# Halves of odd head pairs exchanged, later loads issued by GpSimd, and a new order, in a DeltaNet and MLP-mixer kernel

## The chip, the cores and the metric

The kernel runs on one core of one Trainium2 chip. The metric is the device time of one execution in microseconds (us); less is better. All arithmetic is in fp32.

## The reference

Two blocks one after the other. The first is a DeltaNet attention: four batches, eight heads, 768 positions, head dimension 48. The second is a token and channel mixer on 768 x 384 per batch. The weights of the second come as 64-bit floats and are rounded to fp32 on the chip.

```python
def _attn_ref(q, k, v, beta):
    B, H, S, D = q.shape                      # 4, 8, 768, 48
    k_n = k / (np.linalg.norm(k, axis=-1, keepdims=True) + 1e-06)
    state = np.zeros((B, H, D, D), dtype=np.float32)
    y = np.zeros_like(q)
    for t in range(S):
        kt, vt, bt = (k_n[:, :, t], v[:, :, t], beta[:, :, t, None])
        y[:, :, t] = np.einsum('bhd,bhde->bhe', q[:, :, t], state)
        v_old = np.einsum('bhde,bhd->bhe', state, kt)
        state = state + bt[:, :, :, None] * np.einsum('bhd,bhe->bhde', kt, vt - v_old)
    return y.astype(np.float32)

def _moe_ref(x, w_tok1, w_tok2, w_ch1, w_ch2):
    xt = x.transpose(0, 2, 1)
    h = np.maximum(xt @ w_tok1, 0.0) @ w_tok2        # 768 -> 256 -> 768
    u = x + h.transpose(0, 2, 1)
    h2 = np.maximum(u @ w_ch1, 0.0) @ w_ch2          # 384 -> 1536 -> 384
    return (u + h2).astype(np.float32)
```

## The kernel before

The recurrence is computed in chunks of 64 positions. A batch has 12 chunks, and `recur(t)` is one chunk of all eight heads, 48 steps in all; a unit `u` is 128 positions, two steps, so there are 24 units, six to a batch. The heads are taken as four pairs: the two heads of a pair lie on partitions 0 to 63 and 64 to 127, so that a matmul of one head uses one of the four 64 x 64 quarters of TensorE's array. Which quarter it is follows from the partitions that it reads (one half or the other) and the partitions that it writes.

For every unit there is a preparation, off the chain of steps: `load_kq` loads keys and queries (from unit 12 on as rows, `load_rows` L357, turned by DVE in `turn_rows` L366; and the keys once more in the layout `kst`, by `stacked` L401), `prep` squares kst on ACT (`ksq` L463), makes norms and scales on DVE and ACT, the scaled mask `mb` (L497, GpSimd from unit 4 on) and the scaled keys in `gm` (L514, GpSimd); `grams` multiplies keys with keys and queries (`p_g` L440) and masks the result into `gm` (L443, DVE). `to_parts`, `invert`, `from_parts` and `join` invert the triangular matrices, by way of DRAM from unit 6 on (stores L608, load L655, loads L633; matmuls `p_z` and `p_x` L748, L751, L767). `load_v` loads the values in four DMAs (L401) and scales them on GpSimd (`nrm` L411, `v_st` L414).

A step then does, with the state of the step before: `p_k`, keys times state (L790), eight matmuls of which each takes two passes; `rest` = p_k − v on DVE (L797); `p_y`, queries times state (L810), interleaved with `p_w`, inverse times rest (L814); `w_t`, a copy of p_w, on ACT (L820); `p_s`, the state's increment (L828), interleaved with the second part of `p_y` (L829); `s1`, the new state, on DVE (L837); and two copies of p_y into the mixer's input `xb` on ACT (L842). p_k reads the state of a head on the partitions of this head and writes the partitions of the same or the other half, depending on the parity of the chunk alone, so all its eight matmuls use only two of the four quarters. p_y and p_w use one pair of quarters each, as do p_s and the second p_y. Each of p_k, p_y, p_w and p_s takes one of two rotating PSUM banks; another bank belongs to the warm fillers (`p_warm` L225, L235: matmuls of zeros that keep TensorE running in the start-up).

`mixer(b)` runs when its batch's steps are done: `p_1` (L986), `p_h` (L999), transposes (`p_ut` L1009, copied to `u_t` on ACT, L1013), the first channel product in a plain form for batch 0 (`p_c` L1066) and in a form with 15 instead of 18 block products for the others (`p_r` L958, evacuated by ACT L967 and DVE L970), and the second in a form with seven instead of eight (`p_o` L1088). Its outputs are stored by SP (L1020). The weights are loaded by SP (L271), rounded by ACT, DVE and GpSimd, and kept.

Everything is written as jobs (generators), one for each unit, step, batch and weight block; a string `order` (L1162 and on) lists word by word which job takes its next piece: `k` load_kq, `p` prep, `c` and `d` the two grams, `t` to_parts, `i` invert, `f` from_parts, `j` join, `v` load_v, `r` recur, `m` mixer, `w` weights, `x`, `z` and `Y` fillers. Each engine executes its instructions in this order, and waits only for the tiles (or PSUM banks) that an instruction needs. All DMAs are issued by SP, in this order too, so a DMA that waits for a buffer holds up those behind it.

Of the kernel before, what the change touches and what calls it, by code (L numbers as in the profile page):

```python
# [13 lines left out]
C = 64  # L14
# [9 lines left out]
def kernel(  # L24
# [73 lines left out]
    def ps_seq(shape, name):  # L98
        return psum.tile(shape, FP32, name=name, tag="seq", bufs=2)
# [34 lines left out]
    G = U // HB  # L134
    pads = const.tile([128, 2, NL, H * DP], FP32, name="pads")
# [82 lines left out]

    p_warm = psum.tile([128, 4, 128], FP32, name="p_warm", tag="warm", bufs=1)
# [122 lines left out]
    ranked = set()  # L342
    spread = set()
    keyed = set()

    def load_rows(u, i, src):
# [6 lines left out]
            "(p par) (s g) d -> par s p (g d)", par=2, g=G  # L353
        )
        for par in range(2):
            for r, f in ((C * par, 0), (C * par + HB, HB)):
                nc.sync.dma_start(  # L357
                    out=rows_of[i][r : r + HB, :, 0 : G * D - f], in_=rows[par, :, :, f:]
                )
                if r == C + HB:  # L360
                    spread.add((i, u))
                yield
# [9 lines left out]
    def load_kq(u):  # L372
        b, c = divmod(u, NCH)
        kst = kst_of[slot(u)]
        if u >= TU:
            yield from load_rows(u, 0, k)
            assert last_in(u) in ranked
            yield from stacked(kst, k, u)
            yield from load_rows(u, 1, q)
            return  # L380
        for pad, src in ((kpad, k), (qpad, q)):
# [4 lines left out]
            )  # L386
            yield
            if src is k and u >= RU:
                yield from stacked(kst, k, u)

        heads = kpad[slot(u)].rearrange("t (p par) d -> t p par d", par=2)
        for cc in range(2 if u < RU else 0):
            for par in range(2):
                nc.scalar.copy(kst[PAR[par ^ cc], :, cc], heads[PAR[cc], :, par, 0:D])
                yield

    def stacked(dst, src, u):
        rows = heads_of(src, u)
        for par in range(2):
            for cc in range(2):  # L400
                nc.sync.dma_start(  # L401
# [32 lines left out]
    def grams(u, cc):  # L434
        kqt = kqts[place(u)]
        p_g = ps_prep([128, NP, 2, C], "p_g")
        for p in range(NP):
            for i in range(2):
                f = PAR[i] if u < TU else FEATS[i]
                nc.tensor.matmul(p_g[PAR[i ^ cc], p], kqt[f, p, cc, 0], kqt[f, p, cc])  # L440
            yield
        assert before_in(u) is None or 2 * before_in(u) + cc in walked
        nc.vector.tensor_tensor(  # L443
            out=blocks(gm_of(u))[:, :, cc, D:GW].rearrange(
                "s p (two n) -> s p two n", two=2
            ),
            in0=p_g,
            in1=made[u][:, :, cc, None, :].to_broadcast([128, NP, 2, C]), op=ALU.mult,
        )
        grammed.add((u, cc, False))  # L450
        yield

    def prep(u):
# [7 lines left out]

        ksq = work.tile([128, NB, D], FP32, name="ksq", bufs=1)
# [816 lines left out]
```

## Time and profile before

| | us |
|---|---|
| median of 3 runs | 639.93 (639.85 to 643.66) |
| the profiled execution | 638.03 |
| its span | 636.3 |

The span is the time from the first to the last instruction that the profile shows; 1.7 us of the execution lie around it. The profiled execution is 1.9 us below the median of the runs. The engines are called PE (TensorE), DVE (VectorE), ACT (ScalarE), POOL (GpSimd) and SP (SyncE, which only issues DMAs). PEclk is the granted clock of TensorE as a share of full speed. Where the profile writes "x16" behind a matmul, it counts passes: an fp32 matmul is recorded twice.

### The profile page before, as it was taken

The page shows a single profiled execution, that of the slowest core. Times are in us where ns is not written, and L with a number is a line of the kernel's source. Part 1 is how long each engine was busy: PE and PEld are TensorE (multiplying, and loading weights), DVE is VectorE, ACT ScalarE, POOL GpSimd, SP SyncE. Part 2 cuts the span into 40 slices and gives each one's busy share as a digit, 9 for nine tenths or more (in the row PEclk, how much of TensorE's full clock was granted, in tenths as well). Part 3 has the DMA queues.
Part 4 walks back from the last instruction along what each step waited for, and adds up shares of the span by engine and source line. Part 5 has one row for each costly group of instructions (what it writes and reads, how often), then busy time and mean ns, then how long its engine had stood idle before and what let it go on. Part 6 is the DMA issues. An engine that isn't in the chain of part 4 may idle for free.

```text
span 636.3 us, 21488 instructions
## 1 busy us (share of the span) xinstructions
PE 606.3 (95%) x9132; PEld 529.0 (83%) x9132; DVE 447.3 (70%) x1132; ACT 259.5 (41%) x631; POOL 108.7 (17%) x146
## 2 busy tenths in 40 slices
PE   8488798899999999999999999999999999999997
PEld 5367676667898988958999999769999987999997
DVE  4987876966899568988969987785627253373643
ACT  7758886447422242125623333135244230223240
POOL 2348364235301113021110010101010000000000
PEclk9878997899999999999999999999999999999999
DMA  9787568646442444354444033202020000000000
GB/s 201 131 145 170 138 133 206 151 111 155 104 111 60 92 110 92 81 131 79 92 103 101 13 94 49 66 10 38 2 54 2 27 2 0 26 1 26 1 26 26
DMA packets 135776, 50.27 MB, mean 79 GB/s; under 512 B 114656, under 2 KB 130144, under 8 KB 135680
## 3 DMA queue, kind: packets, MB, share of 16 engines
q1 hardware_dynamic: 135680, 48.89, 34.5%
q8 instruction: 72, 1.18, 0.8%
q14 instruction: 24, 0.20, 0.1%
HBM read 39.42 MB, written 9.44 MB: 77 GB/s over the span
## 4 chain that ended last, share of the span: by engine, by line
PE 81%; DVE 7%; ACT 5%; DMA 3%; issue 2%; SPq 1%; POOL 0%; DVEq 0%; ACTq 0%; POOLq 0%
PE p_o L1088 26%; PE p_r L958 19%; PE p_c L1066 7%; PE p L986 5%; PE p_h L999 5%; PE p_k L790 3%; PE p_s L828 3%; PE p_g L440 3%; PE p_y L810 3%; DMA d<-in_moe_w_ch_dram 1%; PE p_z L748 1%; PE p_ut L1009 1%; PE p_w L814 1%; DVE sub L661 1%; PE p_y L829 1%
## 5 line engine op out<-in xcount | busy, mean ns | idle before, releaser
L1088 PE MATMUL p_o<-wc,r 128*128 128x192 f32 x720 | 125.8, 329 | 0.6 <-ACT u_t L1013 0.6
L1088 PEld LDWEIGHTS p_o<-wc,r 128*128 128x128 f32 x720 | 116.7, 190 | 2.7 <-ACT u_t L1013 1.1
L970 DVE TENSOR_TENSOR r<-r,p_r 128x512 f32<-128x512 f32 x90 | 59.7, 684 | 39.9 <-PE p_r L958 38.8
L1017 DVE TENSOR_TENSOR xb<-xb,p_o 128x192 f32<-128x192 f32 x84 | 29.3, 350 | 59.5 <-PE p_o L1088 59.3
L967 ACT COPY r<-p_r 128x512 f32<-128x512 f32 x54 | 31.5, 584 | 91.4 <-PE p_r L958 89.8
L666 DVE TENSOR_TENSOR x<-x,sub 128x84 f32<-128x84 f32 (+24 forms) x178 | 59.6, 335 | 6.1
L661 DVE TENSOR_TENSOR sub<-x 128x84 f32<-128x84 f32 (+24 forms) x178 | 58.4, 328 | 7.1 <-DMA x<-n_dram 2.8
L1066 PE MATMUL p_c<-u_t,wc 128*128 128x256 f32 x216 | 51.2, 387 | 0.2 <-ACT u_t L1013 0.2
L1088 PE MATMUL p_o<-wc,s 128*128 128x192 f32 x288 | 50.5, 329 | 0.3 <-DVE xb L1017 0.3
L414 POOL TENSOR_TENSOR v_st<-v_st,nrm 128x384 f32<-128x384 f32 x24 | 20.6, 859 | 174.6 <-DMA v_st<-in_v_dram 140.7
L1088 PEld LDWEIGHTS p_o<-wc,s 128*128 128x128 f32 x288 | 46.8, 190 | 1.2 <-DVE xb L1017 0.6
L820 ACT COPY w_t<-p_w 128x192 f32<-128x192 f32 x48 | 15.3, 319 | 73.2 <-PE p_w L814 72.5
L1066 PEld LDWEIGHTS p_c<-u_t,wc 128*128 128x128 f32 x216 | 39.6, 190 | 5.9 <-ACT u_t L1013 0.4
L974 ACT ACTIVATE r<-r 128x512 f32<-128x512 f32 x54 | 33.8, 630 | 25.6 <-DVE r L970 25.3
L440 PE MATMUL p_g<-kq 48*64 48x128 f32 (+1 forms) x704 | 38.3, 290 | 3.3 <-ACT kq L509 3.3
L497 POOL TENSOR_TENSOR mb<-mask_c,cs 128x512 f32<-128x512 f32 x20 | 21.0, 1050 | 114.1 <-DVE gm L443 45.1
L842 ACT ACTIVATE xb<-p_y 64x192 f32<-64x192 f32 x96 | 31.1, 324 | 21.3 <-PE p_y L829 10.5
L958 PE MATMUL p_r<-u_t,wc 128*128 128x128 f32 x288 | 38.5, 277 | 0.0
L958 PE MATMUL p_r<-t_d,wc 128*128 128x128 f32 x288 | 37.2, 280 | 0.0
L443 DVE TENSOR_TENSOR gm<-p_g,mb 128x512 f32<-128x512 f32 x44 | 29.4, 683 | 10.0 <-PE p_g L440 7.2
L986 PE MATMUL p<-xb,w 128*128 128x384 f32 x96 | 35.6, 513 | 0.0
L958 PEld LDWEIGHTS p_r<-u_t,wc 128*128 128x128 f32 x288 | 35.3, 192 | 0.3
(177 smaller groups left out, 1200.1 us busy)
## 6 DMA issues: line engine op xcount, KB each, us to landing
d<-in_moe_w_ch_dram SPq DMA_DIRECT2D x24, 384.0 KB, 3.9
v_st<-in_v_dram SPq DMA_DIRECT2D x96, 48.0 KB, 2.5
out_dram<-xb SPq DMA_DIRECT2D x23, 192.0 KB, 1.9
kst<-in_k_dram SPq DMA_DIRECT2D x64, 48.0 KB, 3.2
n_dram<-gm SPq DMA_DIRECT2D x72, 32.0 KB, 2.4
pads<-in_k_dram SPq DMA_DIRECT2D x24, 96.0 KB, 2.4
pads<-in_q_dram SPq DMA_DIRECT2D x24, 96.0 KB, 2.5
gm<-w_dram SPq DMA_DIRECT2D x72, 32.0 KB, 2.1
```

Source lines behind the costliest of these rows:

```text
L440: nc.tensor.matmul(p_g[PAR[i ^ cc], p], kqt[f, p, cc, 0], kqt[f, p, cc])
L661: nc.vector.tensor_tensor(out=tmp, in0=y[:, :, 0:s, s : s + 1].to_broadcast([n, k, s, w]), in1=y[:, :, s : s + 1, s + 1 : m].to_broadcast( ...
L666: nc.vector.tensor_tensor(out=y[:, :, 0:s, s + 1 : m], in0=y[:, :, 0:s, s + 1 : m], in1=tmp, op=ALU.add,)
L842: nc.scalar.mul(y[:, :, D * i : D * i + D], p_y[PAR[1 - i]], 1.0 if c else -1.0)
L958: nc.tensor.matmul(p[:, i], pieces[i // width][:, at : at + 128], f[f"u{n}"], start=first and i == 0, stop=True, skip_group_check=True,)
L967: nc.scalar.copy(o, p)
L970: nc.vector.tensor_tensor(out=o, in0=o, in1=p, op=ALU.add if sign > 0 else ALU.subtract)
L974: nc.scalar.activation(o, o, ACTF.Relu)
L986: nc.tensor.matmul(p_1[dh], piece_of(w1, c, 0)[:, dh * 128 : (dh + 1) * 128], xb[:, c], start=(c == 0), stop=(c == NCH - 1),)
L999: nc.tensor.matmul(p_h, piece_of(w2, j, c * 128)[:, c * 128 : (c + 1) * 128], r1[j], start=(j == 0), stop=(j == NDH - 1),)
L1066: nc.tensor.matmul(p_c[:, k], piece_of(wc1, cb, f * 128)[:, f * 128 : (f + 1) * 128], u_t[:, cb], start=(cb == 0), stop=(cb == NCB - 1),)
L1088: nc.tensor.matmul(p, a[:, m], wc2[:, m, j], start=(start and i == 0), stop=(i == NM - 1), skip_group_check=True,)
```

## The change

Five things change together.

- **PSUM.** The two rotating banks and the fillers' bank become one tile `seq` of three banks; the fillers write bank 2. For units below 12 p_k, p_w and p_s use bank 1 and p_y bank 0. For units 12 to 23 p_k lies in banks 0 and 1 (even pairs in 0, odd pairs in 1), p_y likewise, p_w in bank 2, p_s in banks 1 (even) and 2 (odd).
- **Exchanged halves.** For units 12 to 23 the two heads of an odd pair change sides in the key and query tiles: `load_rows` writes head and partition half crosswise, in eight DMAs of half the size instead of four. The p_k matmuls of even and odd pairs then lie on different quarters, four in all. The grams, mb (two instructions on halves instead of one, 12 more on GpSimd in all), the layout of gm and the y copies follow this; no other instruction is added.
- **GpSimd issues** the loads of v from unit 6 on (72 DMAs) and those of kst from unit 12 on (48 DMAs), which SP issued before. With the 96 more of load_rows, SP issues 24 fewer DMAs.
- **A new order string**, the same up to the preparation of unit 3 and then sorted anew. It has 21 more filler matmuls (4671 matmuls instead of 4650): seven more of 512 columns, two more of 128, twelve more of the small ones. Some of them stand around the p_k of step 9 (the second pair of lines at the end of the diff; in the first pair, the same place of the old order).
- Assertions on the order (`keys_in`, `pads_in`, `held`), which make no instruction.

```diff
-    def ps_seq(shape, name):
-        return psum.tile(shape, FP32, name=name, tag="seq", bufs=2)
+    seq = psum.tile([128, 3, 512], FP32, name="seq", bufs=1)
+    p_warm = seq[:, 2].rearrange("s (m n) -> s m n", m=4)
+
+    def ps_seq(bank):
+        n = NP * D
+        return seq[:, bank, 0:n].rearrange("s (j odd d) -> s j odd d", odd=2, d=D)
+
+    def ps_split(bank, at):
+        n = NP // 2 * D
+        return seq[:, bank : bank + 2, at * n : at * n + n].rearrange(
+            "s odd (j d) -> s j odd d", d=D
+        )
...
     def load_rows(u, i, src):
-            "(p par) (s g) d -> par s p (g d)", par=2, g=G
-        )
-        for par in range(2):
-            for r, f in ((C * par, 0), (C * par + HB, HB)):
-                nc.sync.dma_start(
-                    out=rows_of[i][r : r + HB, :, 0 : G * D - f], in_=rows[par, :, :, f:]
-                )
-                if r == C + HB:
-                    spread.add((i, u))
-                yield
+            "(j odd par) (s g) d -> odd par s j (g d)", par=2, odd=2, g=G
+        )
+        for odd in range(2):
+            for side in range(2):
+                for r, f in ((C * side, 0), (C * side + HB, HB)):
+                    nc.sync.dma_start(
+                        out=rows_of[i][r : r + HB, odd:NP:2, 0 : G * D - f],
+                        in_=rows[odd, side ^ odd, :, :, f:],
+                    )
+                    if odd and r == C + HB:
+                        spread.add((i, u))
+                    yield
...
     def load_kq(u):
-            yield from stacked(kst, k, u)
+            for n, _ in enumerate(stacked(kst, k, u, nc.sync if u < 12 else nc.gpsimd)):
+                if n == 3:
+                    keys_in.add(u)
+                yield
...
+    def stacked(dst, src, u, queue):
         rows = heads_of(src, u)
         for par in range(2):
             for cc in range(2):
-                nc.sync.dma_start(
+                queue.dma_start(
                     out=dst[PAR[par ^ cc], :, cc], in_=rows[par, cc]
                 )
...
     def load_v(u):
         vsts[u] = v_st = loads.tile([128, NP, 2, D], FP32, name="v_st")
-        yield from stacked(v_st, v, u)
+        yield from stacked(v_st, v, u, nc.sync if u < 6 else nc.gpsimd)
...
     def grams(u, cc):
+        odd = u >= SWAP
         for p in range(NP):
             for i in range(2):
                 f = PAR[i] if u < TU else FEATS[i]
-                nc.tensor.matmul(p_g[PAR[i ^ cc], p], kqt[f, p, cc, 0], kqt[f, p, cc])
-            yield
-        assert before_in(u) is None or 2 * before_in(u) + cc in walked
+                half = cc ^ (odd and p % 2)
+                nc.tensor.matmul(
+                    p_g[PAR[i ^ cc], p], kqt[f, p, half, 0], kqt[f, p, half]
+                )
...
+        out = gm_of(u)[:, :, D:GW]
+        if odd:
+            picked = slice(0, 4, 3) if cc == 0 else slice(1, 3)
+            out = out.rearrange("s (j n) c -> s j n c", n=4)[:, :, picked].rearrange(
+                "s j q (two n) -> s j q two n", two=2
+            )
+            p_g = p_g.rearrange("s (j q) two n -> s j q two n", q=2)
+            mb = sorted_of(made[u])[:, cc, :, :, None, :].to_broadcast(
+                [128, NP // 2, 2, 2, C]
+            )
+        else:
+            mb = made[u][:, :, cc, None, :].to_broadcast([128, NP, 2, C])
...
     def prep(u):
+        if u < SWAP:
+            scaler.tensor_tensor(
+                out=mb, in0=mask_c[:, None, None, :].to_broadcast([128, NP, 2, C]),
+                in1=cs[:, :, :, None].to_broadcast([128, NP, 2, C]), op=ALU.mult,
+            )
+        else:
+            shape = [128, NP // 2, 2, C]
+            of = cs.rearrange("s (j odd) c -> s j (odd c)", odd=2)
+            for cc, picked in enumerate((slice(0, 4, 3), slice(1, 3))):
+                scaler.tensor_tensor(
+                    out=sorted_of(mb)[:, cc],
+                    in0=mask_c[:, None, None, :].to_broadcast(shape),
+                    in1=of[:, :, picked, None].to_broadcast(shape), op=ALU.mult,
+                )
...
     def recur(t):
...
-        heads = [(p, i, PAR[i ^ cc], PAR[1 - i]) for p in range(NP) for i in range(2)]
+        odd = u >= SWAP
+        heads = [
+            (p, i ^ (odd and p % 2), PAR[i ^ cc], PAR[1 - i ^ (odd and p % 2)])
+            for p in range(NP) for i in range(2)
+        ]

         if c > 0:
-            p_k = ps_seq([128, NP, D], "p_k")
+            p_k = ps_split(0, 0) if odd else ps_seq(1)
             for p, i, r, _ in heads:
                 f = FEATS[i]
-                nc.tensor.matmul(p_k[r, p], kqt[f, p, cc, 0], s0[f, p])
-                if i == 1:
+                nc.tensor.matmul(p_k[r, p // 2, p % 2], kqt[f, p, cc, 0], s0[f, p])
+                if r == PAR[1 ^ cc] and (p % 2 or not odd):
                     if p == NP - 1:
                         keyed.add(t)
                     yield
             assert u in scaled
             rest = rest_t
             nc.vector.tensor_tensor(
-                out=rest, in0=p_k, in1=vsts[u][:, :, cc], op=ALU.subtract
+                out=split(rest), in0=p_k, in1=split(vsts[u][:, :, cc]),
+                op=ALU.subtract,
             )
             yield
         else:
             rest = vsts[u][:, :, cc]

         assert u in scaled and u in joined
-        p_y = ps_seq([128, NP, D], "p_y")
-        p_w = ps_seq([128, NP, D], "p_w")
+        p_y = ps_split(0, 2) if odd else ps_seq(0)
+        p_w = ps_seq(2 if odd else 1)
         for p, i, r, o in heads:
             if c > 0:
                 f = FEATS[i]
                 nc.tensor.matmul(
-                    p_y[o, p], kqt[f, p, cc, 1], s0[f, p],
-                    start=(p == 0), stop=False,
+                    p_y[o, p // 2, p % 2], kqt[f, p, cc, 1], s0[f, p],
+                    start=(p == 0 or odd and p == 1), stop=True,
+                    skip_group_check=True,
                 )
-            nc.tensor.matmul(p_w[r, p], gm[r, 2 * p + cc, TC], rest[r, p])
-            if c == 0 and i == 1 and p < NP - 1:
+            nc.tensor.matmul(p_w[r, p // 2, p % 2], gm[r, 2 * p + cc, TC], rest[r, p])
+            if c == 0 and r == PAR[1 ^ cc] and p < NP - 1:
                 yield
         if cc == 1:
             asked.add(u)
         yield
-        nc.scalar.copy(w_t, p_w)
+        nc.scalar.copy(split(w_t), p_w)
         yield

         on = c < NQ - 1
         if on:
-            p_s = ps_seq([128, NP, D], "p_s")
+            p_s = ps_split(1, 3) if odd else ps_seq(1)
         for p, i, r, o in heads:
             if on:
-                nc.tensor.matmul(p_s[PAR[i], p], gm[r, 2 * p + cc, 0:C], w_t[r, p])
+                nc.tensor.matmul(
+                    p_s[PAR[i], p // 2, p % 2], gm[r, 2 * p + cc, 0:C], w_t[r, p],
+                    start=(not odd or p % 2 == 1 or c == 0 and p == 0), stop=True,
+                    skip_group_check=True,
+                )
             nc.tensor.matmul(
-                p_y[o, p], gm[r, 2 * p + cc, GC], w_t[r, p],
-                start=(c == 0 and p == 0), stop=(p == NP - 1),
+                p_y[o, p // 2, p % 2], gm[r, 2 * p + cc, GC], w_t[r, p],
+                start=(c == 0 and p == 0),
+                stop=True, skip_group_check=True,
             )
         walked.add(t)
         yield
         if on:
             if c > 0:
-                nc.vector.tensor_tensor(out=s1, in0=s0, in1=p_s, op=ALU.subtract)
+                nc.vector.tensor_tensor(
+                    out=split(s1), in0=split(s0), in1=p_s, op=ALU.subtract
+                )
             else:
-                nc.vector.tensor_copy(out=s1, in_=p_s)
-            yield
-        for i in range(2):
+                nc.vector.tensor_copy(out=split(s1), in_=p_s)
+            yield
+        y = y.rearrange("s (j odd) (i d) -> s j (odd i) d", odd=2, i=2)
+        for e in range(2):
+            if odd:
+                picked = slice(0, 4, 3) if e == 0 else slice(1, 3)
+            else:
+                picked = slice(e, 4, 2)
             nc.scalar.mul(
-                y[:, :, D * i : D * i + D], p_y[PAR[1 - i]], 1.0 if c else -1.0
+                y[:, :, picked],
+                p_y[PAR[1 - e]],
+                1.0 if c else -1.0,
             )
...
     order = """
...
-    w29 w27*2 r8*2 w29*3 j4*2 r8 w22*4 t9*4 r8*3 p10 h5*2 k11 p9 r8 h5 r9 h5 j5
-    r9*4 w4 i2*2 p10 i2*2 v5 i2 v5 w19 m0 r9 k10 j5 p10 i2 p10 v5 i2*2 w15 w4 v5*2
...
+    w22 t8*3 r8*5 p10 w7 j4*2 w29*2 h5*4 r8*2 w29*2 t9*4 w22*2 p10 v6 r8 w4 Y r8
+    r9*2 j5 Y w4*2 p11*2 r9*3 p10*2 z i2 v5 h5 i2 x r8 r9*2 p10 r9 i2*5 z j5 r9
...
```

More of the change, by code (lines that the diff above doesn't have):

```diff
@@ L342 @@
     ranked = set()
+    keys_in = set()
+    pads_in = set()
+    held = {"t11": None, "zst": None}
     spread = set()
@@ L386, in load_kq @@
             )
+            pads_in.add((pad is kpad, u))
             yield
             if src is k and u >= RU:
-                yield from stacked(kst, k, u)
+                for n, _ in enumerate(stacked(kst, k, u, nc.sync if u < 12 else nc.gpsimd)):
+                    if n == 3:
+                        keys_in.add(u)
+                    yield
         heads = kpad[slot(u)].rearrange("t (p par) d -> t p par d", par=2)
@@ L870, in block_of @@
             return w_block(j, k)
+        for u in range(NL, WIDE):
+            assert slot(u) < NL or u in ranked and turned.issuperset([(True, u), (False, u)])
         a = {(j, k): (j, k) for j in range(3) for k in range(NCB)}
```

177 lines of the change are left out of this document (92 added, 85 removed).

## The prediction

> **What bounds the kernel now.** I read the page first: the busy line, then the slices with the granted clock.
>
> ```profile
> span 636.3 us, 21488 instructions
> PE 606.3 (95%) x9132; PEld 529.0 (83%) x9132; DVE 447.3 (70%) x1132; ACT 259.5 (41%) x631; POOL 108.7 (17%) x146
> PEclk9878997899999999999999999999999999999999
> ```
>
> PE is busy for 95% of the span, and the clock falls below 9 tenths only in the first 120 us or so. Then the busy time by stretches (columns: stretch, its length, then PE, PEld, DVE, ACT, POOL, the clock, DMA share, GB/s):
>
> ```profile
> 160.00:240.00 80.00, 79.95 (x1352) 70.53 (x1347) 64.39 (x163) 26.37 (x70) 12.95 (x17) 1.00 0.42 96
> 240.00:320.00 80.00, 79.60 (x1325) 66.83 (x1324) 71.37 (x174) 29.35 (x75) 14.74 (x19) 1.00 0.43 93
> 320.00:400.00 80.00, 80.00 (x1101) 76.66 (x1100) 64.54 (x169) 26.85 (x61) 7.08 (x12) 1.00 0.32 72
> ```
>
> From 160 us to 400 us PE idles 0.45 us in all. There only two things change the time: PE work that is removed, and a new wait that PE cannot fill. The start is another matter:
>
> ```profile
> 98.00:100.00 2.00, 1.04 (x37) 0.75 (x32) 0.72 (x3) 1.84 (x5) 0.98 (x2) 1.00 0.83 225
> 100.00:102.00 2.00, 1.46 (x49) 1.30 (x50) 0.72 (x2) 1.72 (x5) 1.10 (x2) 0.54 0.53 146
> 102.00:104.00 2.00, 1.54 (x36) 1.29 (x33) 1.05 (x4) 1.17 (x4) 1.58 (x3) 0.50 0.89 251
> 104.00:106.00 2.00, 2.00 (x8) 1.58 (x7) 1.07 (x6) 0.85 (x3) 0.52 (x2) 0.50 0.90 235
> 106.00:108.00 2.00, 2.00 (x39) 0.96 (x39) 1.76 (x8) 0.38 (x2) 0.00 (x0) 0.75 1.00 268
> ...
> 116.00:118.00 2.00, 1.53 (x60) 1.40 (x53) 1.83 (x6) 1.66 (x4) 0.00 (x0) 0.81 0.94 282
> 118.00:120.00 2.00, 2.00 (x36) 1.91 (x32) 1.93 (x7) 0.69 (x3) 0.35 (x1) 0.50 1.30 186
> 120.00:122.00 2.00, 2.00 (x19) 1.09 (x20) 1.94 (x4) 0.00 (x0) 1.02 (x2) 0.84 0.92 220
> ```
>
> A gap in PE's work at 98 us is followed by about half the clock, and PE then needs 2.28 us for what takes 1.49 us at full clock, as the chain that ended last shows:
>
> ```profile
> 89.87 5.33 DMA d<-in_moe_w_ch_dram
> 96.11 3.89 DMA d<-in_moe_w_ch_dram
> ...
> 105.11 2.28 PE p L986 x4
> ...
> 109.24 1.49 PE p L986 x4
> ...
> 122.96 0.67 PE p_y L829 x16
> ```
>
> The chain's pieces before the gap are loads of weights; its p_y at 122.96 is the last of step 11, the end of the first batch.
>
> **Keys times state (p_k) on four quarters.** The trace gives both prices. p_k alone, on two quarters, then the four-quarter p_y and p_w of a step (start, duration, what):
>
> ```profile
> 297.52 0.67 PE L790 MATMUL p_k<-s_t,kq 48*64 48x48 f32 x16
> 298.12 0.38 PE L958 MATMUL p_r<-t_d,wc 128*128 128x128 f32 x1
> ```
> ```profile
> 293.01 0.25 PE L810 MATMUL p_y<-s_t,kq 48*64 48x48 f32 x1
> ...
> 293.48 0.22 PE L814 MATMUL p_w<-rest,gm 64*64 64x48 f32 x1
> 293.62 0.25 PE L748 MATMUL p_z<-t,gm 32*32 32x32 f32 x4
> ```
>
> Sixteen passes (8 matmuls, two each) take 298.12 − 297.52 = 0.60 us on two quarters; 32 take 293.62 − 293.01 = 0.61 us on four. The 0.60 us are 8 rounds of about 58 ns and an entry and exit; four quarters need 4 rounds, so a p_k becomes 4 × 0.058 = 0.23 us shorter. The exchange acts in steps 24 to 47, of which 24 and 36 start a batch and have no p_k: 22 × 0.23 = 5.1 us at most. Not all of it is free: in the old order seven pairs of p_g matmuls ran in the quarters that p_k left empty:
>
> ```profile
> 302.30 0.28 PE L790 MATMUL p_k<-s_t,kq 48*64 48x48 f32 x4
> 302.37 0.28 PE L440 MATMUL p_g<-kq 48*64 48x128 f32 x2
> 302.41 0.28 PE L790 MATMUL p_k<-s_t,kq 48*64 48x48 f32 x4
> ```
>
> The p_g passes (302.37 and 302.48) follow each other every 0.11 us in a quarter, so such a pair, two passes in each of two quarters, hid 0.22 us beside p_k: 1.5 us for seven. With the other small shifts of the order (changes between tile sizes, p_g passes beside each other) the row prices summed over every matmul but the fillers give **−3.2 us**. The p_g, p_y, p_w and p_s matmuls keep their number and quarters: nothing. Only their places in PSUM change.
>
> **New waits in steps 24 to 47.** p_k now writes banks 0 and 1, where p_y and p_s of the step before lie. So ACT's two y copies wait for DVE's s1 (bank 1 is shared), and the next p_k waits for both y copies; before, s1 alone had to be done. The old rows, all engines in one stretch:
>
> ```profile
> 301.58 0.22 PE L829 MATMUL p_y<-w_t,gm 64*64 64x48 f32 x1
> ...
> 301.85 0.35 DVE L837 TENSOR_TENSOR s_t<-s_t,p_s 128x192 f32<-128x192 f32 x1 [0.17 <-PE p_y L829]
> ...
> 301.89 0.66 ACT L842 ACTIVATE xb<-p_y 64x192 f32<-64x192 f32 x2 [1.39 <-PE p_y L829]
> ```
>
> From the last p_y pass: 0.27 us to s1, 0.35 us in it, 0.05 us to ACT, 0.66 us for two copies, some 0.06 us to PE: 1.39 us, where 0.68 us were needed. What covers it is the PE work between the last p_y and the next p_k. In the new order it is short in eight places: before step 31 eight p_g matmuls on uneven quarters (0.66 us by 0.11 us a pass), before 37 and 44 a p_z/p_x block, before 29 sixteen p_g (0.88 us), before 40, 41, 42 and 45 four p_r matmuls. Their rows in the chain:
>
> ```profile
> 289.40 1.09 PE p_r L958 x8
> ...
> 293.69 0.62 PE p_z L748 x32
> ```
>
> With entry and exit these cover 0.72, 0.77 (twice), 0.94 and 1.24 (four times); the rest have over 1.6 us. Stalls: 0.67 + 0.62 + 0.62 + 0.45 + 4 × 0.15 = **+2.9 us**, if ACT and DVE are free at that moment. Below that, 0 if the bank wait falls away; above, 5 us if DVE's queue (89% busy in 240 to 320 us) makes s1 late. Queued on ACT behind a waiting y copy are r and w_t copies, which PE waits for. The old order's own stalls in this part, **−0.5 us** (the 0.45 above), go.
>
> **GpSimd's loads.** 120 loads (72 of v, 48 of kst) leave SP for POOL, and load_rows has 96 more, half as large, on SP. SP's longest waits are those of the stores for their data, which lie in the dense part:
>
> ```profile
> SPq L1020 <- DVE xb L1017: 202.1, 15, 44.2
> ```
>
> PE waited for no load there, so SP's relief is worth nothing and the extra row loads, hidden in these 202 us, cost nothing. At the start, where SP's queue is full, unit 12 alone brings eight of them:
>
> ```profile
> L357 SPq DMA_DIRECT2D pads<-in_k_dram x48: 312/430/1340, 111.6 to 345.9; - x48
> ```
>
> 8 × 0.43 = 3.4 us more stand against about 16 loads of v and kst that leave SP there (9.8 us at the 0.61 us of the row below): SP gains some 6 us, and the weights' loads keep their places in its queue. POOL issues no DMA in the old trace, so the price is bounded by rows of both engines (min/median/max ns):
>
> ```profile
> L411 POOL TENSOR_TENSOR nrm<-nrm,eps x24: 191/200/647, 52.2 to 471.6; 128x8 f32<-128x8 f32 x24
> ```
> ```profile
> L497 POOL TENSOR_TENSOR mb<-mask_c,cs x20: 1038/1042/1204, 29.0 to 377.6; 128x512 f32<-128x512 f32 x20
> ```
> ```profile
> L401 SPq DMA_DIRECT2D kst<-in_k_dram x64: 601/615/1512, 15.2 to 351.0; - x64
> ```
> ```profile
> kst<-in_k_dram SPq DMA_DIRECT2D x64, 48.0 KB, 3.2
> ```
>
> The ends are 0.20 and 1.20 us; I take SP's 0.62, the same load on the nearest queue. The last row has the landing, 3.2 us. It matters because ksq, kst's reader, stands in ACT's queue ahead of w_t and y. Laying POOL's queue out by these prices, kst is on time in seven of the twelve units; in five (14 to 17, 22) it lands 0.3 to 3 us late, since two v loads and four kst loads follow a late buffer release in one burst. ACT has 0 to 2 us of room after ksq: it runs some 2 us late in all, half of which I let reach PE: **+1.0 us** (0 at 0.30 us an issue, 8 at 1.05). mb in two halves costs POOL about 0.2 us a unit (its row against nrm's), hidden at 17% busy. The "DMA: Bandwidth & Descriptors" page of the Trainium skill, section "Latency and other measured facts", puts the first byte of GpSimd's DMAs at about 1 us against 0.6 for SP's; by it the term would be near 2, an estimate; no run shown yet can tell.
>
> **The new order at the start.** Up to step 11 the same work is due, DVE and ACT with 1 us more ahead of it. It has more warm fillers, of which the block around p_k of step 9 falls where the gap at 98 us was. The clock lost there is 2 × (0.46 + 0.50 + 0.50 + 0.25) = 3.4 us, at 116 us 2 × (0.19 + 0.50 + 0.16) = 1.7. As other chains (weights, DVE) end near there too, I take half: **−2.5 us** (bounds −5 and +3, if the fillers and the order only delay).
>
> **Sum.** 638.0 us (profiled execution: span 636.3 and 1.7 around it) − 3.2 + 2.9 − 0.5 + 1.0 − 2.5 = 635.7. The median of the runs shown lies 1.9 above that execution: 637.6, so I say 637.5.
>
> **Rivals.**
> 1. Faster: y copies and kst come in time and the start keeps its clock: 637.5 − 2.9 − 1.0 − 2.5 = 631. For it: ACT was only 34 to 37% busy from 240 to 400 us. Against: the covers above are counts of PE work, not guesses. 29%.
> 2. Slower: POOL's issue is dear, 1.2 us or so. kst then lands 3 to 9 us late in six units, ACT blocks by over 20 us in all, half reaches PE: 637.5 + 11.5 = 649. It starts above 0.65 us an issue and passes the 1% bound at about 1.1. For it: the bursts, ACT's strict order. Against: nrm's 0.20 us shows a light POOL instruction. 21%.
> 3. Issues that wait out a DVE instruction, half of this row's 684 ns more each:
>
> ```profile
> L970 DVE TENSOR_TENSOR r<-r,p_r 128x512 f32<-128x512 f32 x90 | 59.7, 684 | 39.9 <-PE p_r L958 38.8
> ```
>
> That is 0.96 an issue, 5 us more at PE: 642.5. Against it, mb stays at 1038 to 1204 ns beside a DVE at 80 to 89%. 6%. This is a rule of the Trainium skill ("SBUF — State Buffer", section "SBUF: two separate sides"): GpSimd cannot write descriptors while VectorE holds their shared port. By that rule it would come out so; the mb row shows little such blocking.
> 4. The change doesn't do what it says: two banks and exchanged halves leave p_k at 0.60 us. 637.5 + 5.1 − 1.5 = 641. Against it is p_y and p_w's row. 6%.
>
> **How the numbers follow.** The forecast has the remaining 38%. About 1% (6.4 us) is what a measurement of this kernel can tell from no change: below 633.5 is faster, above 646.3 slower. Faster: most of rival 1 and a tenth of the forecast's spread, 0.32. Slower: most of rival 2, with tails of 3 and the forecast, 0.26. Same: 0.42. The forecast's own range is 633 to 643; the range over the cases reaches down to rival 1 and 2 us of start beyond it, 629, and up to rival 2, 650.
>
> **What would show it.** p_k's 16 passes within some 0.37 us when alone; PE idle released by the y copy ahead of p_k, in the eight places; POOL DMAs near 0.6 us, and ACT's ksq waiting for kst by at most 3 us; a clock of 1.00 between 100 and 108 us. I am wrong if ksq waits add up to over 10 us, if s1 comes late behind DVE's queue, or if the end of step 11 (now 123.6 us) moves by more than 5 us.

## The result and the profile after

| | before | after |
|---|---|---|
| median (4 runs each, on one chip) | 641.77 us (639.85 to 643.66) | 673.62 us (673.12 to 677.18) |
| ratio to before, 95% interval | | 1.0494 [1.045, 1.0538] |
| the profiled execution, its span | 638.03, 636.3 | 673.12, 671.3 |

The change made the kernel 5% slower. The busy line and the clock of the page after, against those of before:

```profile
span 671.3 us, 21763 instructions
PE 624.0 (93%) x9174; PEld 534.0 (80%) x9174; DVE 449.5 (67%) x1132; ACT 259.3 (39%) x631; POOL 183.6 (27%) x278
PEclk9978969599999999979999999999999999999999
```

PE has 17.7 us more busy time and 17.3 us more idle time. To see where, I cut both spans at the same two events: the end of the y copies of step 11 (the last of batch 0) and of step 23. Before, then after (columns: stretch, length, busy PE, PEld, DVE, ACT, POOL, the clock, DMA share, GB/s):

```profile
0.00:124.30 124.30, 99.57 (x2261) 78.76 (x2262) 97.27 (x253) 88.09 (x234) 54.73 (x75) 0.90 0.76 160
124.30:248.40 124.10, 123.18 (x1988) 102.78 (x1988) 95.08 (x237) 49.88 (x128) 28.07 (x34) 1.00 0.46 105
248.40:636.30 387.90, 383.60 (x4886) 347.47 (x4884) 254.92 (x644) 121.58 (x270) 25.88 (x37) 1.00 0.19 45
```
```profile
0.00:142.60 142.60, 118.34 (x2305) 87.58 (x2306) 95.87 (x257) 90.47 (x240) 58.92 (x82) 0.87 0.63 138
142.60:269.00 126.40, 122.45 (x1984) 102.14 (x1983) 99.82 (x234) 47.75 (x121) 63.68 (x97) 1.00 0.48 108
269.00:671.30 402.30, 383.22 (x4888) 344.26 (x4886) 253.80 (x643) 121.03 (x270) 60.98 (x101) 0.99 0.18 42
```

The 35.0 us are +18.3 at the start, +2.3 in steps 12 to 23 and +14.4 in the rest. At the start PE idles as long as before (24.3 us, length less busy; 24.7 before) but is busy 18.8 us longer. 13.2 us of that are the fillers, which keep it busy for 31.1 us instead of 17.9 (passes that overlap counted once); the remaining 5.6 us go with a lower clock (0.87 for 0.90) and were not taken apart. In the rest it is busy as long as before and idles 19.1 us instead of 4.3.

What PE waits for stands in the groups of p_k, before and after (busy time and mean ns; idle time of PE just before the group, and what ended it), and in the waits after (us in total, times, longest):

```profile
L790 PE MATMUL p_k<-s_t,kq 48*64 48x48 f32 x656 | 28.0, 226 | 1.3 <-DVE s_t L837 0.9 <-ACT xb L842 0.4
```
```profile
L859 PE MATMUL seq<-s_t,kq 48*64 48x48 f32 x656 | 23.9, 229 | 18.7 <-ACT xb L925 18.0 <-DVE s_t L913 0.6
```
```profile
ACT xb L925 <- DVE s_t L913: 47.1, 20, 13.4
PE seq L859 <- ACT xb L925: 18.4, 20, 5.8
ACT xb L925 <- DMA out_dram<-xb: 10.0, 1, 10.0
```

p_k is 4.1 us cheaper, as intended, but PE now waits 18 us for ACT's y copies ahead of it, and the y copies wait for s1 on DVE. The prediction expected such waits where units 12 to 23 share a bank, from step 24 on. They are there earlier. This is the timeline at the end of step 13 (unit 6), where p_y lies in bank 0 and p_s and p_k in bank 1:

```profile
169.62 0.35 DVE L913 TENSOR_TENSOR s_t<-s_t,seq 128x192 f32<-128x192 f32 x1 [1.89 <-PE seq L904]
...
170.01 0.66 ACT L925 ACTIVATE xb<-seq 64x192 f32<-64x192 f32 x2 [1.29 <-DVE s_t L913]
...
170.72 0.26 PE L859 MATMUL seq<-s_t,kq 48*64 48x48 f32 x2 [0.60 <-ACT xb L925]
```

The y copy reads another bank than s1, and both only read `seq`; still it starts 0.04 us after s1 ends. p_k writes another bank than the copy reads, and still starts 0.05 us after the second copy. The order is that of the tile `seq` as a whole. This is no single case: of the 96 y copies of the kernel before, 26 run while an s1 runs; of the 96 of the changed kernel, none does.

At the start this takes in the fillers, which are now in the same tile. From the chain that ended last:

```profile
116.25 0.36 DVE rest L866
...
116.65 2.52 PE seq L234 x4
...
119.19 0.33 ACT xb L925
```

Fillers (L234), meant for a time in which PE has nothing to do, wait for rest on DVE, then take 2.52 us, and a y copy waits for them. In the first of these two stretches of 2 us PE idles for 1.54 us, in the second its clock is 0.50 (after; the last column but two is the clock):

```profile
114.00:116.00 2.00, 0.46 (x24) 0.32 (x16) 0.59 (x3) 1.41 (x4) 1.13 (x2) 0.96 0.13 50
116.00:118.00 2.00, 1.35 (x2) 0.83 (x3) 1.81 (x8) 0.47 (x2) 0.37 (x2) 0.50 0.00 0
```

At step 24, the first of a batch, the chain after shows the largest single gap:

```profile
291.15 0.36 DVE xb L1104
291.53 2.76 DMA out_dram<-xb
...
294.39 0.33 ACT xb L925
294.73 0.33 ACT xb L925
...
295.11 0.68 PE seq L859 x16
```

The y copies of step 24 write the xb buffer whose last store must land first. Before, the same wait was ACT's alone (its timeline):

```profile
271.84 0.66 ACT L842 ACTIVATE xb<-p_y 64x192 f32<-64x192 f32 x2 [7.73 <-DMA out_dram<-xb]
```

After, p_k of step 25 stands behind these copies: PE idles from 289.36 to 295.11, 5.75 us, and the clock falls to 0.83 in 280 to 300 us.

### The profile page after: what moved, and what is told of

Its sections match the earlier page's. It is cut to its first block, busy times and chain, and to the rows that moved or that the text cites. A ratio compares the mean times of both kernels' runs of the same rounds, so it can differ in the third digit from the quotient of the medians.

```text
span 671.3 us, 21763 instructions
## 1 busy us (share of the span) xinstructions
PE 624.0 (93%) x9174; PEld 534.0 (80%) x9174; DVE 449.5 (67%) x1132; ACT 259.3 (39%) x631; POOL 183.6 (27%) x278
## 4 chain that ended last, share of the span: by engine, by line
PE 69%; DVE 11%; ACT 6%; DMA 2%; issue 2%; SPq 0%; POOL 0%; DVEq 0%; ACTq 0%
PE p_o L1175 19%; PE p_r L1045 17%; PE p_c L1153 7%; PE p L1073 6%; PE p_h L1086 5%; PE seq L880 3%; ACT xb L925 3%; PE seq L859 2%; PE seq L899 2%; DVE sub L717 2%; DVE x L722 2%; PE p_g L465 2%; PE p_z L805 1%; PE seq L904 1%; DVE r L1127 1%
## 5 line engine op out<-in xcount | busy, mean ns | idle before, releaser
L424 POOL DMA_DIRECT2D v_st<-in_v_dram x72 | 44.7, 625 | 97.2 <-DVE rest L866 72.7
L925 ACT ACTIVATE xb<-seq 64x192 f32<-64x192 f32 x96 | 31.2, 325 | 89.3 <-DVE s_t L913 47.1
L1061 ACT ACTIVATE r<-r 128x512 f32<-128x512 f32 x54 | 33.9, 631 | 25.3 <-DVE r L1057 24.7
L859 PE MATMUL seq<-s_t,kq 48*64 48x48 f32 x656 | 23.9, 229 | 18.7 <-ACT xb L925 18.0
L859 PEld LDWEIGHTS seq<-s_t,kq 48*64 48x64 f32 x656 | 18.5, 137 | 27.0 <-ACT xb L925 22.6
L1073 PE MATMUL p<-xb,w 128*128 128x384 f32 x96 | 38.2, 551 | 0.0
L465 PEld LDWEIGHTS p_g<-kq 48*64 48x64 f32 (+1 forms) x704 | 28.6, 139 | 11.8 <-ACT kq L565 7.2
L293 POOL TENSOR_TENSOR wc<-w_f,d 128x384 uint32<-128x384 uint32 x24 | 24.6, 1028 | 47.4 <-DVE w_f L289 15.8
```

The source lines that it names most:

```text
L424: queue.dma_start(out=dst[PAR[par ^ cc], :, cc], in_=rows[par, cc])
L465: nc.tensor.matmul(p_g[PAR[i ^ cc], p], kqt[f, p, half, 0], kqt[f, p, half])
L859: nc.tensor.matmul(p_k[r, p // 2, p % 2], kqt[f, p, cc, 0], s0[f, p])
L925: nc.scalar.mul(y[:, :, picked], p_y[PAR[1 - e]], 1.0 if c else -1.0,)
L1061: nc.scalar.activation(o, o, ACTF.Relu)
L1073: nc.tensor.matmul(p_1[dh], piece_of(w1, c, 0)[:, dh * 128 : (dh + 1) * 128], xb[:, c], start=(c == 0), stop=(c == NCH - 1),)
```

## The experiments

Twelve kernels, in three groups. Each ratio is to the kernel before, run beside the group on the same chip (medians 641.59, 639.53 and 641.50 us); times of different groups are compared with these differences in mind. "The start" is the time up to the end of step 11, and the three stretches are cut as above.

**Which part of the change: the tile, the order, or the rest?** The first group crosses them. The kernel before with its sequence banks put into one tile (and, as in the changed kernel, `stop` set on every p_y matmul):

```diff
+    seq = psum.tile([128, 3, 512], FP32, name="seq", bufs=1)
+    p_warm = seq[:, 2].rearrange("s (m n) -> s m n", m=4)
...
-        return psum.tile(shape, FP32, name=name, tag="seq", bufs=2)
+        bank = 0 if name == "p_y" else 1
+        return seq[:, bank, 0 : NP * D].rearrange("s (p d) -> s p d", p=NP)
```

> The old kernel and old order with one edit: the two rotating banks and the fillers' bank become one tile of three banks (p_y in bank 0, p_k, p_w and p_s in bank 1, fillers in bank 2). Bank by bank nothing conflicts that did not before. Theory A: this alone makes it slower by 10 to 30 us, 652 to 672, with PE waiting ahead of p_k for the y copies in more than ten steps. Theory B and C: 640 to 645.

Measured: 667.79 us, 1.0421 [1.0392, 1.0449]. Its p_k group and its stretches:

```profile
L792 PE MATMUL seq<-s_t,kq 48*64 48x48 f32 x656 | 29.3, 227 | 18.2 <-ACT xb L844 18.0
```
```profile
0.00:128.80 128.80, 100.09 (x2252) 77.50 (x2252) 98.03 (x253) 88.12 (x235) 54.68 (x75) 0.91 0.74 156
128.80:260.50 131.70, 125.64 (x1996) 103.81 (x1997) 95.25 (x237) 50.16 (x127) 30.25 (x37) 1.00 0.44 98
260.50:665.00 404.50, 388.62 (x4886) 349.38 (x4884) 255.93 (x644) 121.62 (x270) 23.28 (x35) 0.99 0.19 43
```

One tile alone, with the old order, old halves and old queues, costs 26.2 us, and puts the same 18.0 us of waiting for the y copies before p_k; none of its 96 y copies runs while an s1 runs. The loss lies elsewhere than in the changed kernel: 4.5 us at the start, 7.6 in steps 12 to 23 and 16.6 in the rest, where PE is also busy 5.0 us longer, at a clock of 0.99 for 1.00. The edit also moved p_y and p_w to fixed banks, so p_k, p_w and p_s follow each other in one bank; in the order of a step they do so anyway, through rest, w_t and s1. The kernels with three tiles, below, have the fixed banks and the `stop` too: the first loses nothing in steps 12 to 23, and one in the old order has the start of before. Up to step 23 the tile is what is left.

The other way round, the changed kernel with three separate tiles up to step 23 (from step 24 on the split over two banks needs the one tile):

```diff
-    seq = psum.tile([128, 3, 512], FP32, name="seq", bufs=1)
-    p_warm = seq[:, 2].rearrange("s (m n) -> s m n", m=4)
...
+    banks = [early.tile([128, 512], FP32, name=f"seq{i}") for i in range(3)]
+    p_warm = banks[2].rearrange("s (m n) -> s m n", m=4)
```

> The new kernel and new order, but the three banks are three tiles up to step 23 and become the one tile at step 24, where the exchange begins; no instruction is added. Theory A: the start and steps 12 to 23 get back most of what they lost (18 + 2 us in the profiles): 652 to 660 us. Theory B: the start stays long: 668 to 674. Theory C: 670 to 674.

Measured: 662.12 us (656.18 to 665.75), 1.0335 [1.0255, 1.0416], 11.5 us less than the changed kernel. Its first two stretches:

```profile
0.00:130.70 130.70, 113.16 (x2305) 85.61 (x2306) 96.26 (x255) 90.12 (x240) 58.69 (x81) 0.91 0.69 151
130.70:253.90 123.20, 122.77 (x1984) 102.46 (x1984) 100.10 (x237) 47.69 (x122) 63.39 (x96) 1.00 0.49 111
```

The start loses 11.9 us of its 18.3, and steps 12 to 23 are 0.9 us shorter than before the change. The rest stays (403.3 us). Up to step 23 19 y copies run while an s1 runs, from step 24 on, in the one tile, none.

The order alone, in the code of before (SP issuing everything):

```diff
-    w29 w27*2 r8*2 w29*3 j4*2 r8 w22*4 t9*4 r8*3 p10 h5*2 k11 p9 r8 h5 r9 h5 j5
...
+    j4*2 w29*2 h5*4 r8*2 w29*2 t9*4 w22*2 p10 v6 r8 w4 Y r8 r9*2 j5 Y w4*2 p11*2
...
```

> The old kernel's code (old PSUM tiles, no exchange, SP issues all loads) with the new order of the pieces; where a job has more pieces in the new kernel, two of them are one here. Theory A (one tile): in the new kernel p_k, p_y, p_w, p_s and the fillers are parts of one PSUM tile, and the built program makes p_k wait for the y copies and the y copies for s1 in nearly every step from 1 on, not only from 24 on, and makes two fillers wait for DVE's rest; the order is harmless without these waits: 638 to 645 us. Theory B (order): the new order alone, with its 12 us of additional fillers before step 11, makes the start longer: 655 to 662 us, step 11 ending near 140 us instead of 124. Theory C (GpSimd's loads come late): as A for this kernel, about 641.

Measured: 703.09 us, 1.0961 [1.0923, 1.0998], slower than the whole change. Taken by itself this would convict the order. ACT's waits say otherwise:

```profile
ACT ksq L463 <- DMA kst<-in_k_dram: 65.9, 7, 18.8
```

The order is made for kst loads that don't queue on SP: with SP alone they come 65.9 us late in all. The run can't price the order; the second group gives it its queue.

And the changed code in the old order (two pieces of the grams set a little later, and the row loads twice as many):

```diff
-    r9*2 j5 Y w4*2 p11*2 r9*3 p10*2 z i2 v5 h5 i2 x r8 r9*2 p10 r9 i2*5 z j5 r9
...
+    r8 w22*4 t9*4 r8*3 p10 h5*2 k11 p9 r8 h5 r9 h5 j5 r9*4 w4 i2*2 p10 i2*2 v5 i2 v5
...
```

> The new kernel's code with the old order (the pieces of a load of rows doubled, two gram pieces set back by a few words, as the exchange needs it). Theory A: the waits remain, in an order that was not laid out for them: 655 to 675 us, with step 11 ending 8 to 18 us later than in the old kernel. Theory B: the start is as in the old kernel (124 us), and only the stalls from step 24 on remain: 645 to 652 us. Theory C: 665 or more, with ksq or v_st waiting over 10 us for GpSimd's loads.

Measured: 674.39 us, 1.0512 [1.0466, 1.0559], like the changed kernel, but differently made: its start is 132.8 us instead of 142.6, its steps 12 to 23 139.0 instead of 126.4. Two things cancel, which the second group takes apart.

**The second group: order, queue and exchange apart.** First, the old code with the new order, and GpSimd issuing as in the change:

```diff
-            yield from stacked(kst, k, u)
+            yield from stacked(kst, k, u, nc.gpsimd)
...
-        yield from stacked(v_st, v, u)
+        yield from stacked(v_st, v, u, nc.sync if u < 6 else nc.gpsimd)
```

> The old code (two rotating banks, own bank for fillers, no exchange) with the new order, and GpSimd issuing the loads of v from unit 6 and of kst from unit 12, as the new kernel does. Against e1_old_code_new_order (703) it shows what the new issue queue does in the new order. Theory A with C turned round (the order was laid out for two queues, and SP alone is late with kst): 638 to 648, the start some 6 us longer than in the old kernel and no stalls from step 24 on. Theory B: over 655.

Measured: 642.31 us (10 runs), 1.0035 [1.0014, 1.0055]. Order and queue together cost 0.35%, 2.8 us by the medians. The same queue in the old order (lines against the kernel above):

```diff
-    j4*2 w29*2 h5*4 r8*2 w29*2 t9*4 w22*2 p10 v6 r8 w4 Y r8 r9*2 j5 Y w4*2 p11*2
...
+    w29 w27*2 r8*2 w29*3 j4*2 r8 w22*4 t9*4 r8*3 p10 h5*2 k11 p9 r8 h5 r9 h5 j5
...
```

> The old kernel and old order with one edit: GpSimd issues the loads of v from unit 6 and of kst from unit 12. Theory A: 638 to 643, no change that can be measured, kst in time. Theory C: over 648, ACT's ksq waiting for kst in several units.

Measured: 652.43 us, 1.0204 [1.0159, 1.0249]. The chain shows how a moved load fails (start, duration, what):

```profile
157.66 1.01 POOL wc L284
158.67 0.57 POOL v_st L401
159.24 3.50 DMA kst<-in_k_dram
...
162.76 0.53 ACT ksq L463
...
163.32 0.55 DVE ksum L466
163.87 0.27 DVE s_t L837
...
164.19 0.34 PE p_k L790 x2
```

In POOL's queue kst stands behind a weight's rounding and a load of v. It lands late, ksq holds up ACT, ksum delays s1 on DVE, and PE idles 4.33 us. So queue and order belong together: each alone costs far more (652.43 and 703.09) than the pair (642.31).

Then the changed kernel with three tiles at the start, and three pieces of mixer(1) moved ahead of p_k of step 25, to cover the wait for the stores:

```diff
-    m0*2 i4*3 m0 i4 m0 i4 r24*4 j13 r24*3 m0 i4*3 m0*2 i4*2 p18 m0 r24 j13 r25*2
-    p18 k19 m1*3 p18 m1 k19*2 i4*4 m1*2 r25 k19*2 i4 r25 i4*2 k18*3 k19 i4*2 k19 i4
+    p18 m0 r24 j13 m1*3 r25*2 p18 k19 p18 m1 k19*2 i4*4 m1*2 r25 k19*2 i4 r25 i4*2
```

> The kernel with three tiles up to step 23, and in its order three pieces of the second mixer (4 us of p matmuls) moved ahead of step 25's p_k. Theory D (the store): at step 24 the y copies go into a buffer whose last stores are still under way; in the old kernel nothing on PE waited for these copies, now p_k of step 25 does, and PE idles 5.8 us there and loses clock behind it. Then this gains 4 to 7 us against e1_new_three_tiles_start: 655 to 658. If the idle only moves to the next wait: no gain, 660 to 663.

Measured: 650.20 us (648.88 to 651.71), 1.0167 [1.0139, 1.0196], 11.9 us less again, of which 2.1 may be the chips' (their kernels before differ by that). Only 3.8 us are the repair: the gap before p_k of step 25 shrank from 5.9 to 2.04 us, and the stretch after step 23 from 403.3 to 399.5. The start, in which nothing changed, was 126.9 us in this profile for 130.7, and the remaining 4 lie between the profiled executions and their medians (659.27 for 662.12, 651.71 for 650.20). So the length of one and the same start moves by about 4 us from profile to profile; a third kernel with it had 129.5.

This kernel and the old code with the new order and queue now differ by the exchange, the tile it needs from step 24 on, and the three moved pieces. Their p_k groups, each with its last stretch:

```profile
L877 PE MATMUL seq<-s_t,kq 48*64 48x48 f32 x656 | 23.1, 227 | 8.1 <-ACT xb L943 7.8 <-DVE s_t L931 0.2
...
250.20:649.70 399.50, 384.08 (x4888) 345.16 (x4886) 253.66 (x643) 121.10 (x271) 62.73 (x102) 0.99 0.17 42
```
```profile
L790 PE MATMUL p_k<-s_t,kq 48*64 48x48 f32 x656 | 27.1, 221 | 1.2 <-DVE s_t L837 1.0
...
250.20:639.50 389.30, 384.63 (x4888) 348.25 (x4886) 254.03 (x643) 121.43 (x270) 60.65 (x96) 1.00 0.17 44
```

Four quarters save 4.0 us of p_k's busy time but only 0.55 us of PE's. The clock takes the rest back, as far as an estimate goes. In windows of 1 us it falls to 0.50 twice in this stretch, for three windows each, behind gaps of PE of 2.04 us (ending at 276.49) and 2.30 us (ending at 383.30); 1 less the clock, summed over the windows, is 1.7 us each time, 3.4 together, and 3.45 are missing. Behind a gap of 2.19 us (ending at 525.18) it stays at 1.00, and in the old code it is 1.00 up to 630 us. PE's idle time (length less busy) rises from 4.7 to 15.4 us. The exchange, with its tile, costs 7.9 us by the medians.

Last, the changed code with three tiles at the start, in the old order:

```diff
-    p_warm = seq[:, 2].rearrange("s (m n) -> s m n", m=4)
+    p_warm = banks[2].rearrange("s (m n) -> s m n", m=4)
...
+    r8 w22*4 t9*4 r8*3 p10 h5*2 k11 p9 r8 h5 r9 h5 j5 r9*4 w4 i2*2 p10 i2*2 v5 i2 v5
```

> The new code with the old order (as e1_new_code_old_order, 674) and three tiles up to step 23. Theory A: the start returns to the old kernel's 124 us, and what is left is the exchange's stalls from step 24 on: 648 to 658. Theory B has the same for the start but nothing for steps 12 to 23; if the start stays at 132 us, something else in the new code delays it.

Measured: 659.05 us, 1.0304 [1.0277, 1.0332]. The start is 123.3 us, that of before; steps 12 to 23 take 131.8 us, as with the same queue in the old code (131.3). So of the two things that cancelled, the longer start was the tile's, and most of the longer steps 12 to 23 the queue's in the old order. Against the same queue in the old order without exchange (652.43), the exchange costs 6.6 us by the medians, so it has a price in that order too.

**The third group: fillers, and a repair.** Are the fillers in the tile enough to explain the start? Fillers in a tile of their own up to step 23, banks 0 and 1 in one:

```diff
...
+    two = early.tile([128, 2, 512], FP32, name="seq2")
+    banks = [two[:, i] for i in range(2)]
+    p_warm = early.tile([128, 4, 128], FP32, name="p_warm")
```

> The new kernel with the fillers in a PSUM tile of their own up to step 23, banks 0 and 1 still one tile (p_k still waits for the y copies from step 1 on). It splits what three tiles gave (673.6 to 662). If the fillers' waits for DVE's rest are the larger part: 660 to 664. If p_k's waits for the y copies are: 668 to 674.

Measured: 666.91 us, 1.0387 [1.0348, 1.0427]; the start is 134.6 us, between 142.6 with one tile and 130.7 with three. Both parts count; by the medians the fillers' place is worth 6.7 us (673.62 to 666.91) and the two banks 4.8 more (to 662.12). The split is rough: the runs of the kernel with three tiles spread over 9.6 us, and the profiles put the banks' part at 3.9 us of the start and 3.2 of steps 12 to 23. With banks 0 and 1 in one tile again no y copy runs while an s1 runs.

Could the wait be mended by order? The y copies of ten steps from 24 on put directly behind s1, and one more piece of mixer(1) ahead of p_k of step 25 (lines against the kernel with p_k of 25 later):

```diff
-    p18 m0 r24 j13 m1*3 r25*2 p18 k19 p18 m1 k19*2 i4*4 m1*2 r25 k19*2 i4 r25 i4*2
+    p18 m0 j13 m1*4 r25*2 p18 k19 p18 k19*2 i4*4 m1*2 r25 k19*2 i4 r25 i4*2 k18*3
```

> The kernel e2_three_tiles_pk25_later with one more mixer piece ahead of step 25's p_k, and from step 24 on the y copies' place in ACT's order moved to directly behind s1 (ten steps), so that they no longer stand behind copies of p_r, which wait for later PE work. Theory E (ACT's order): the 9 us of PE idle left from step 28 on are mostly y copies in the wrong place of ACT's queue: 642 to 646. If they are the length of the chain itself (s1, two copies): 648 to 651.

Measured: 655.37 us, 1.0226 [1.018, 1.0272]: a miss, above both times expected. It was aimed at rows like these of the kernel with p_k of 25 later (timeline of all engines):

```profile
523.10 0.69 DVE L1075 TENSOR_TENSOR r<-r,p_r 128x512 f32<-128x512 f32 x1 [1.10 <-PE p_r L1063]
523.82 0.63 ACT L1079 ACTIVATE r<-r 128x512 f32<-128x512 f32 x1 [1.10 <-DVE r L1075]
524.47 0.66 ACT L943 ACTIVATE xb<-seq 64x192 f32<-64x192 f32 x2
...
525.18 0.45 PE L877 MATMUL seq<-s_t,kq 48*64 48x48 f32 x16 [2.19 <-ACT xb L943]
```

The y copies stand in ACT's queue behind a Relu that waits for DVE, so p_k waits 2.19 us for work of the mixer. That gap went, but gaps of 1.97 us (281.47, ahead of p_y) and 1.86 us (416.98, ahead of p_k) came in its place, and the stretch from step 23 on kept its length (400.1 for 399.5 us).

Without the fillers that the new order has in steps 6 to 9, on this kernel and on the old code with the new order and queue:

```diff
-    j4*2 w29*2 h5*4 r8*2 w29*2 t9*4 w22*2 p10 v6 r8 w4 Y r8 r9*2 j5 Y w4*2 p11*2
+    w29*2 h5*4 r8*2 w29*2 t9*4 w22*2 p10 v6 r8 w4 r8 r9*2 j5 w4*2 p11*2 r9*3 p10*2
```

> As e3_pk25_later_y_early, without the six filler pieces between the steps 6 and 10. If the fillers cost more than the clock that they hold: 1 to 5 us less than that kernel. If they hold the clock: 1 to 5 us more.

> The old code with the new order and GpSimd's loads (642.3), without the same six filler pieces: 636 to 641 if these cost more than they hold, which would beat the old kernel or be level with it; 643 to 647 if they hold the clock.

Measured: 655.43 us, 1.0221 [1.0178, 1.0265], and 641.59 us (10 runs), 1.0008 [0.9984, 1.0032]. As separate tiles these fillers neither help nor cost. The second kernel is level with before; no version beat it.

Undone step by step the change reads: 673.6 us as made, 662.1 with three tiles at the start, 650.2 with p_k of step 25 later, 642.3 without the exchange and its tile, 641.6 without the late fillers; as ratios to the kernel before, 1.0494, 1.0335, 1.0167, 1.0035 and 1.0008. Within the scatter of the start, the second step is worth 4 to 12 us.

## Why the prediction was wrong

**The step that failed** is "New waits in steps 24 to 47", and under it this sentence of the part on p_k: "The p_g, p_y, p_w and p_s matmuls keep their number and quarters: nothing. Only their places in PSUM change." The places were the change that mattered. I took waits to go bank by bank, so that nothing would change before step 24, and priced eight short covers at 2.9 us (the terms add up to 2.96). The execution is 37.4 us longer than the sum's 635.7: about 20.8 of them lie in the start, 2.3 in steps 12 to 23, for which I had no term, and 14.2 in the rest. The runs show waits by tile, in three places:

- *Start.* The term was −2.5 us, it came to +18.3. With separate tiles it is +2.6 to +6.9: seven kernels with the new order have 126.9 to 131.2 us, three with the old order 123.1 to 124.3. So the larger part is the tile's, and the sign was wrong without it too. The fillers to which I gave a gain took more of PE's time than the gaps they were to fill (those of 512 columns up to step 11, before and after), and leaving the late ones out, with separate tiles, changed nothing:

```profile
L225 PE MATMUL p_warm<-warm 128*128 128x512 f32 x20 | 11.3, 694 | 0.0
```
```profile
L234 PE MATMUL seq<-warm 128*128 128x512 f32 x34 | 21.4, 763 | 2.2 <-DVE rest L866 2.2
```

- *Step 24.* My condition "if ACT and DVE are free at that moment" looked at busy shares. ACT was not busy, it was waiting for a store, 7.73 us in the trace that I had. A copy that waited beside PE's work became one that PE waits for.
- *Steps 25 to 47.* The stretch after step 23 idles 14.8 us more (19.1 for 4.3), 5.75 of it at step 25. Nine are left, where I had 2.9 − 0.5. The largest that I followed, 2.18 us at 544.66, is the case quoted above: y copies late behind the mixer's in ACT's strict queue, which no count of PE work between p_y and p_k shows.

**Keys times state** was right. p_k alone on four quarters, in the kernel with p_k of 25 later (timeline of PE):

```profile
362.30 0.40 PE L877 MATMUL seq<-s_t,kq 48*64 48x48 f32 x16
362.62 1.08 PE L1193 MATMUL p_o<-wc,r 128*128 128x192 f32 x5
```

That is 0.32 us from the one to the next, against 0.60 before; the steps' mean saving is 4.0 / 22 = 0.18 us where I had 0.23. Rival 4 falls. The net gain, −3.2, is not seen in PE's busy time (−0.55 in the same order); by the estimate above, the clock took it back.

**GpSimd's loads** were right in the price of an issue, and near it in the wait. Their rows after (min/median/max ns), the landing (median us), and what ksq waits for on ACT (us in total, times):

```profile
L424 POOL DMA_DIRECT2D v_st<-in_v_dram x72: 617/617/780, 111.1 to 493.3; - x72
L424 POOL DMA_DIRECT2D kst<-in_k_dram x48: 617/617/650, 132.9 to 375.7; - x48
```
```profile
v_st<-in_v_dram POOLq DMA_DIRECT2D x72, 48.0 KB, 2.6
kst<-in_k_dram POOLq DMA_DIRECT2D x48, 48.0 KB, 2.7
```
```profile
DMA kst<-in_k_dram: 5.7, 2
```

0.617 us against the 0.62 taken; rivals 2 and 3 fall. ksq waits 5.7 us in two places (1.0 and 4.7 us) where I had five units; the sum is under the 10 named as the sign of error, the longer wait over the 3 that I expected at most. The same queue and order in the old code gave 642.3, 2.8 us over before with a start 3.2 us longer, so no run shows the +1.0 by itself. mb in halves costs 2 × 0.617 for 1.042 us before, 0.19 us a unit, as taken.

Rival 1 is refuted: the y copies hold PE up and the start did not keep its clock; only kst came nearly in time. None of the rivals held the case: the slower one was put on GpSimd's price, not on the tile. That the time came out nearer to it than to the forecast is chance. The signs listed at the end did point to it: the end of step 11 moved by 18.3 us, over the 5 named, and PE's idle time before p_k is released by the y copies.

What stays open: from step 24 on the exchange shares banks too, so that there the runs don't tell the tile's waits from the banks'; waits truly bank by bank were not tried. That needs s1, rest and the y copies split by bank, which adds instructions on DVE and ACT; that the exchange would gain then is not shown.

## What to carry to other kernels

When buffers that rotated on their own become slices of one tile, list every reader and writer of the tile on every engine, and assume that they run in program order until a timeline row shows two of them overlapping; then price the waits from step one, not only where addresses meet. A wait that an engine off the path sits through today (here 7.73 us of ACT for a store) is the first price to look up when something on the path is put behind that engine. And undo parts in pairs: an order and the queue that it was made for cost 9.6% and 2.0% apart, and 0.35% together.

## What was not expected of the hardware

- GpSimd issues a 48 KB load in the same 617 ns nearly every time (maximum 780), while DVE is busy for 79% of 142.6 to 269 us (99.82 of 126.40). The Trainium skill, "SBUF — State Buffer", section "SBUF: two separate sides", says that GpSimd cannot write descriptors while VectorE holds the shared port; these rows show no delay over 0.16 us. How much of DVE's busy time holds that port no row tells, so this doesn't speak against the rule. Nor did its loads land later than SP's: 2.6 us for v and 2.7 for kst, where SP's own v and kst, earlier in the same profile, take 3.2 and 2.9.
- A pause of PE of 2.19 us (ending at 116.65) is followed by a clock of 0.50, at which a block of four filler passes takes 2.52 us on the chain. Here fillers that were themselves late ran at the low clock that they were to prevent. Pauses of much the same length differ in what follows: 2.04 and 2.30 us were followed by 0.50 in the kernel with p_k of 25 later, 2.19 us by 1.00.
